# Attention into a gated MLP on one core: outputs of the first and last batch go straight into the MLP's activation tiles, in a newly planned order

## The chip, the cores and the metric

The kernel runs on one NeuronCore of a Trainium2 chip. The metric is the device time of one launch in microseconds (us). Before the change three runs gave 876.30, 876.43 and 876.82 us; the median is 876.43 us.

## The reference

Queries are averaged in pairs of neighbouring positions (1152 positions become 576), attention runs over 4 batches of 8 heads, and the attention outputs, laid out as 2304 tokens of 512 features, go through an MLP with a gate. All is fp32.

```python
q_pool = q.reshape(B, H, S // 2, 2, D).mean(axis=3)          # B, H, S, D = 4, 8, 1152, 64
scores = (q_pool @ k.transpose(0, 1, 3, 2)) / np.sqrt(D)
attn = np.exp(scores - scores.max(-1, keepdims=True))
attn = attn / (attn.sum(-1, keepdims=True) + 1e-9)
x = (attn @ v).transpose(0, 2, 1, 3).reshape(B * S // 2, H * D)   # 2304 x 512
h = x @ w_in                                                  # 512 x 2048
out = (h * np.clip(h + 3, 0, 6) / 6) @ w_out                  # 2048 x 512
```

## The kernel before, in words

**Attention.** Two heads form a pair; there are 16 pairs g (four to a batch), and each is done in two halves h of 288 queries. (15, 1) is thus the second half of the last pair. For a half, TensorE makes the scores (`pv<-qh,kT` for the first five pairs, `pqk` later), ScalarE copies them to SBUF (`s`), VectorE keeps a running maximum (`m`), the maximum is folded and spread over TensorE (`pst`), VectorE subtracts it (`s<-s,pst`, L685), ScalarE takes the exponential (L693), and TensorE multiplies with the values (`pav`, L710). The sums of the exponentials of later pairs are added on GpSimd in four steps for each of the two heads (`d`, L703: two of 864 columns, two of 288); VectorE then folds them (`dh`, L723), TensorE sums over partitions (`psr<-dh,same`, L730, function `sums`), and VectorE inverts, widens and multiplies (`divide`, L781). The result `x` is split into a high part `xh` on ScalarE (L786) and a remainder `xl` on GpSimd (L789), since all matmuls of the MLP work with a high and a low part.

**The way to the MLP.** Each half's `xh` and `xl` (128 x 288) are stored in DRAM (`spill`, L795). The MLP works on chunks of 256 tokens, held feature by feature in `mxh` and `mxl` (`do_load_x`, L382: two loads of 512 KB). The last 768 tokens are done after the attention: a chunk of 256 and a tile `last` of 512 tokens, which `load_last` (L911) fills from DRAM, one pair at a time.

**The MLP.** For each chunk and each of 16 blocks f of the hidden width: `layer` (12 matmuls of 256 columns into `ph`, L392), relu on ScalarE (L397), gate on VectorE (L401), a high part on ScalarE (`gh`, L405) and a remainder on GpSimd (`gl`, L410), and `project` (6 matmuls of 512 columns into `po`, L425). The weights come from `w_d`, where an early conversion put them, two tiles per block (L375), three buffers for each. The second phase's first matmuls need the PSUM that the first five pairs free (the step `second`).

**What sets the order.** `arrange` lists all steps with their needs, buffers, costs and a due place; `Order.run` walks through time with these costs and writes each engine's instructions down in the order it found. On the chip each engine, and the SP queue, which issues nearly all DMAs, follows its own list strictly. START to STICK are the numbers that place the steps.

Of the kernel before, what the change touches and what calls it, by code (L numbers as in the profile page):

```python
# [21 lines left out]
SWEEPS = ((0, 0, 8), (1, 0, 8), (0, 8, 16), (1, 8, 16), (2, 0, 16), (3, 0, 16), (4, 0, 16), (5, 0, 16))  # L22
START = (265.37, 174.4, 333.68, 473.16, 315.93, 125.77, 294.83, 251.1)
SLOPE = (-22.5, 5.61, -19.51, -1.68, 18.53, 29.67, 8.1, 10.68)
LAG = 95.37
MLP = (-455.8, 178.11, 154.5, -337.97)
CONV = 489.51
CSTEP = (779.1, 171.15)
NEAR = 5
EARLY = 5  # L30
FCV = 12
BIAS = (-499.81, -337.54, 74.41, -260.87, -123.47, 36.52)
CUT = 8
PER = (11.97, 20.48)
AT = (268.28, -145.28, 1.89, 285.13, -233.93, 261.99, -360.51, 263.48, 186.09, 367.06, 25.71, -87.67, -226.55, 320.99)
ATL = (21.71, -3.97, -191.36, 678.02, 338.19, 328.75, 109.71, -429.46, 291.22, 244.53, 587.93, 369.41, 499.12, 174.71)
TAIL = 768
STICK = 0.2249
CT = 256
# [8 lines left out]
class Order:  # L48
# [5 lines left out]
    def add(self, key, place, cost, fn, needs=(), takes=(), frees=()):  # L54
        assert key not in self.key, key
        self.key[key] = len(self.steps)
        self.steps.append((round(1e4 * place), cost, fn, tuple(needs), tuple(takes), tuple(frees)))

    def run(self):
# [10 lines left out]
        back, out, t, wires = [], [], 0.0, 0.0  # L70
# [10 lines left out]
        while len(out) < len(steps):  # L81
# [4 lines left out]
            for e in engines:  # L86
# [53 lines left out]
            if not began:  # L140
# [3 lines left out]
                t = min(later)  # L144
        return [(steps[n][2], e) for _, n, e in out]


def arrange(od, do, B=4, NPAIR=4, KT=9, KC=3, NH=2, NFC=16, NT=2304, P=128, HQ=288, SQ=576):
    add = od.add
    chunks = range(0, NT - TAIL, CT)  # L150
    NG, C3 = B * NPAIR, range(KT // KC)

    def place(g):
        return PER[0] * min(g, EARLY) + PER[1] * max(g - EARLY, 0)


    for g in range(NG):
# [34 lines left out]
        for h in range(NH):  # L192
# [75 lines left out]
            add(("dv", g, h), z + at[9], {"DVE": (370, 450)}, do("divide", g=g, h=h), [("rb" if late else "qu", g, h), ("ev", g, h)], (), ("av",))  # L268
            add(("xh", g, h), z + at[10], {"ACT": (340, 420)}, do("split_x", g=g, h=h), [("dv", g, h)], ("xo",))
            add(("xl", g, h), z + at[10], {"POOL": (800, 820)}, do("split_x", g=g, h=h), [("xh", g, h)], (), ("x",))  # L270
            add(("sp", g, h), z + at[10] + 1, {"SP": (940, 5800, 1000)}, do("spill", g=g, h=h), [("xl", g, h)], (), ("xo",))
        add(("lv", g), lead + at[13], {"SP": (470, 5200, 1750)}, do("load_v", g=g), [("lk", g)], ("vr",))
# [18 lines left out]

    def spills(c0, c1):
        return [("sp", b * NPAIR + p, h) for b in range(B) for h in range(NH)
                for p in range(NPAIR) if b * SQ + h * HQ < c1 and b * SQ + (h + 1) * HQ > c0]

    hd = w0 = w1 = pj = None
    after = lambda *keys: [x for x in keys if x]
    for i, (c, f0, f1) in enumerate(SWEEPS):
        for f in range(f0, f1):
            m, first, last = (c, f), f == f0, f == f1 - 1  # L300
            z = START[i] + SLOPE[i] * (f - f0)
            if f == 0:
                add(("lx", c), z - 5, {"SP": (940, 7500, 3100)}, do("do_load_x", c=c), spills(c * CT, (c + 1) * CT), ("mx",))
# [4 lines left out]
            add(("hd", m), z, {"PE": (1440, 1660, 0, "m")}, do("do_layer", m=m), [w0, ("lx", c), ("second",)] + after(hd),  # L308
                ("h",), ("w0",) + (("mx",) if f == NFC - 1 else ()))
# [3 lines left out]
            add(("gh", m), z + MLP[2], {"ACT": (300, 408)}, do("do_upper", m=m), [("ga", m)], ("g",))  # L313
            add(("gl", m), z + MLP[3], {"POOL": (700, 740)}, do("do_lower", m=m), [("gh", m)], (), ("r6",))
# [11 lines left out]
    c = len(chunks)  # L326
    add(("lx", c), place(NG) + 7, {"SP": (940, 7500, 3100)}, do("do_load_x", c=c), spills(c * CT, (c + 1) * CT), ("mx",))
    for p in range(NPAIR):
        add(("ll", p), place(NG - NPAIR + p + 1) + 12, {"SP": (940, 6000, 1550)}, do("load_last", p=p),
            [("sp", NG - NPAIR + p, gr) for gr in range(NH)] + [("sw", NFC - 1, h) for h in range(2)] + ([("ll", p - 1)] if p else []))  # L330
    add(("end", 0), 1e4, {"PE": (1440, 1660, 0, "m")}, do("nothing"), [("lx", c), pj])
    add(("end", 1), 1e4, {"PE": (2730, 2950, 0, "m")}, do("nothing"), [("ll", NPAIR - 1), ("end", 0)])


@with_exitstack
def pooled_attention_then_gated_mlp(ctx, tc, q, k, v, w_in, w_out, out):
# [128 lines left out]
    with ExitStack() as a:  # L465
# [317 lines left out]
        def split_x(eng, g, h):  # L783
            if eng == "ACT":
                xo_t[g, h] = [xo.tile([P, HQ], F32R, tag=t, name=t) for t in ("xh", "xl")]
                nc.scalar.copy(out=xo_t[g, h][0], in_=x_t[g, h])  # L786
            else:
                xh, xl = xo_t[g, h]
                by[eng].tensor_tensor(out=xl, in0=x_t.pop((g, h)), in1=xh.bitcast(F32), op=ALU.subtract)  # L789
# [110 lines left out]
        def do_write(eng, c, t, last):  # L900
# [83 lines left out]
```

## Time and profile before

| | us |
|---|---|
| median of three runs | 876.43 |
| the profiled execution, whole time | 872.62 |
| its span, first to last instruction | 870.8 |
| TensorE (PE) busy | 836.6 |
| VectorE (DVE) busy | 673.8 |
| ScalarE (ACT) busy | 572.3 |
| GpSimd (POOL) busy | 497.8 |

The profiled execution lies 3.8 us under the median. The records call a matmul busy until its result is out, and matmuls overlap, so a busy PE can hide gaps of a fraction of a microsecond. The chain of work that ended last is 74% PE, 12% DVE, 4% DMA, 4% ACT, 4% issue and 2% POOL.

### The profile page before, as it was taken

To read this page: it belongs to the slowest core of one execution; us is meant where nothing else is said; L and a number is where in the kernel's file an instruction comes from. 1 tells how busy PE (TensorE), PEld (TensorE's weight loads), DVE (VectorE), ACT (ScalarE), POOL (GpSimd) and SP (SyncE) were. 2 spreads that over 40 slices of the span, in tenths; PEclk is the share of its full clock that TensorE was granted. 3 is DMA by queue.
4 is the path that set the end of the run, shared out by engine and by line. 5 is a ranking of instruction groups with operands and counts; after the bars stand their busy time and mean duration, and the time that the engine had idled before them with its cause. 6 is when DMAs were issued, how large, how long until landed. Compare 5 with 4: busy or idle time off the path is not lost.

```text
span 870.8 us, 16256 instructions
## 1 busy us (share of the span) xinstructions
PE 836.6 (96%) x5668; PEld 650.8 (75%) x5668; DVE 673.8 (77%) x1330; ACT 572.3 (66%) x1206; POOL 497.8 (57%) x437
## 2 busy tenths in 40 slices
PE   4899999999999999999999999999999999999997
PEld 3445555578878877888887887788888867888886
DVE  3899999998988999988888998899988772222222
ACT  3779889886777777766667876687776652222222
POOL 1658776656777685947686878659684592000000
PEclk9799999999999999999999999999999999999999
DMA  9979586799886868997767778996867678443423
GB/s 239 317 216 285 187 269 227 228 278 361 261 290 219 277 219 255 300 300 267 236 210 240 264 240 259 323 290 207 273 217 244 210 267 269 141 132 117 139 98 95
DMA packets 114545, 206.06 MB, mean 237 GB/s; under 512 B 44576, under 2 KB 68128, under 8 KB 114464
## 3 DMA queue, kind: packets, MB, share of 16 engines
q1 hardware_dynamic: 113776, 203.65, 72.8%
q10 hardware_dynamic: 688, 1.38, 0.6%
q8 instruction: 45, 0.74, 0.3%
q14 instruction: 36, 0.29, 0.1%
HBM read 173.02 MB, written 31.98 MB: 235 GB/s over the span
## 4 chain that ended last, share of the span: by engine, by line
PE 74%; DVE 12%; DMA 4%; ACT 4%; issue 4%; POOL 2%; SPq 1%; DVEq 0%; POOLq 0%; ACTq 0%
PE ph L392 20%; PE po L425 15%; PE pav L710 13%; PE pqk L614 10%; PE pt L425 5%; DVE m L632 4%; PE pv L610 3%; DVE s L685 3%; DMA w<-w_d 2%; ACT s L519 1%; PE pt L588 1%; PE pt L554 1%; PE psr L740 1%; ACT s L693 1%; DMA w_d<-scratch 1%
## 5 line engine op out<-in xcount | busy, mean ns | idle before, releaser
L693 ACT ACTIVATE s<-s 128x864 f32<-128x864 f32 x192 | 177.4, 932 | 21.1 <-DVE s L685 19.0
L392 PE MATMUL ph<-mxmxh,w 128*128 128x256 f32 x896 | 183.1, 287 | 3.3 <-DVE r L401 2.6
L685 DVE TENSOR_TENSOR s<-s,pst 128x864 f32<-128x864 f32 x168 | 174.0, 1042 | 0.4
L519 ACT COPY s<-pqk 128x288 f32<-128x288 f32 x396 | 145.3, 402 | 29.2 <-PE pqk L614 26.2
L710 PE MATMUL pav<-s,vr 128*64 128x288 f32 x1152 | 153.2, 411 | 0.0
L392 PEld LDWEIGHTS ph<-mxmxh,w 128*128 128x128 f32 x896 | 147.6, 192 | 7.3 <-DVE r L401 4.3
L632 DVE TENSOR_TENSOR m<-pqk,m 128x288 f32<-128x288 f32 x308 | 138.0, 448 | 14.8 <-ACT s L519 8.4
L425 PE MATMUL po<-w,gh 128*128 128x512 f32 x448 | 140.1, 394 | 0.0
L397 ACT ACTIVATE r<-ph,three 128x256 f32<-128x256 f32 (+1 forms) x128 | 63.9, 499 | 114.8 <-PE ph L392 110.2
L392 PE MATMUL ph<-mxmxl,w 128*128 128x256 f32 x448 | 127.3, 284 | 0.5 <-DMA mxmxl<-xl_d 0.5
L401 DVE SCALAR_TENSOR_TENSOR r<-r,ph 128x256 f32<-128x256 f32 (+1 forms) x128 | 57.2, 447 | 85.5 <-ACT r L397 84.4
L614 PE MATMUL pqk<-qh,kT 128*128 128x288 f32 x396 | 119.8, 316 | 1.5 <-DVE m L632 0.7
L410 POOL TENSOR_TENSOR gl<-r,gh 128x256 fp32r<-128x256 f32 x96 | 71.4, 745 | 86.9 <-ACT gh L405 70.6
L710 PEld LDWEIGHTS pav<-s,vr 128*64 128x64 f32 x1152 | 77.3, 136 | 57.6 <-issue 9.2
L703 POOL TENSOR_TENSOR d<-s 128x864 f32<-128x864 f32 x44 | 90.6, 2059 | 42.7 <-ACT s L693 42.1
L614 PE MATMUL pqk<-ql,kT 128*128 128x288 f32 x396 | 111.8, 294 | 0.0
L425 PEld LDWEIGHTS po<-w,gh 128*128 128x128 f32 x448 | 84.9, 189 | 14.5
L425 PE MATMUL po<-w,gl 128*128 128x512 f32 x224 | 90.7, 405 | 2.5 <-DMA w<-w_d 2.5
L703 POOL TENSOR_TENSOR d<-d,s 128x864 f32<-128x864 f32 x44 | 90.3, 2052 | 2.9 <-ACT s L693 1.5
L392 PEld LDWEIGHTS ph<-mxmxl,w 128*128 128x128 f32 x448 | 86.0, 192 | 1.7 <-DMA mxmxl<-xl_d 0.8
L614 PEld LDWEIGHTS pqk<-qh,kT 128*128 128x128 f32 x396 | 74.7, 189 | 12.4 <-DVE m L632 3.9
L405 ACT CAST gh<-r 128x256 fp32r<-128x256 f32 (+1 forms) x128 | 55.8, 436 | 37.4 <-DVE r L401 28.0
(104 smaller groups left out, 1412.8 us busy)
## 6 DMA issues: line engine op xcount, KB each, us to landing
w<-w_d SPq DMA_DIRECT2D x224, 512.0 KB, 5.9
w_d<-scratch SPq DMA_DIRECT2D x32, 512.0 KB, 5.6
kr<-in_k_dram SPq DMA_DIRECT2D x32, 288.0 KB, 4.9
vr<-in_v_dram SPq DMA_DIRECT2D x16, 576.0 KB, 4.4
qr<-in_q_dram SPq DMA_DIRECT2D x15, 576.0 KB, 5.6
raw<-in_moe_w_in_dram SPq DMA_DIRECT2D x16, 512.0 KB, 4.7
raw<-in_moe_w_out_dram SPq DMA_DIRECT2D x16, 512.0 KB, 6.0
xh_d<-xh SPq DMA_DIRECT2D x32, 144.0 KB, 4.9
```

The lines of the kernel that those rows point to most:

```text
L392: nc.tensor.matmul(ps, w[:, wi, cs], x[:, c, :], start=(m == 0), stop=(m == 3 * NCC - 1))
L397: nc.scalar.activation(out=r6, in_=ps, func=AF.Relu, bias=three)
L401: nc.vector.scalar_tensor_tensor(out=out, in0=r6, scalar=6.0, in1=ps, op0=ALU.min, op1=ALU.mult)
L410: on.tensor_tensor(out=gl, in0=r6, in1=gh.bitcast(F32), op=ALU.subtract)
L425: nc.tensor.matmul(o, g[:, ts], w[:, wi, :], start=(first and n == 0), stop=(last and n == 2))
L519: nc.scalar.copy(out=out, in_=in_)
L614: nc.tensor.matmul(ps[:, 0:HQ], kT[g][:, j, t, :], w[:, j, :], start=(m == 0), stop=(m == 1))
L632: nc.vector.tensor_tensor(out=m, in0=ps, in1=s0 if t == 1 else m, op=ALU.max)
L685: by[eng].tensor_tensor(out=s, in0=s, in1=m.unsqueeze(1).to_broadcast([P, KC, HQ]), op=ALU.subtract)
L693: nc.scalar.activation(out=s, in_=s, func=AF.Exp, scale=SCALE)
L703: by[eng].tensor_tensor(out=out, in0=x, in1=y, op=ALU.add)
L710: nc.tensor.matmul(av_t[g, h][j * D:(j + 1) * D, :], vr_t[g][:, j, t, :], s_t[g, h][:, j, t, :], start=(t == 0), stop=(t == KT - 1),)
```

## The change

`routes` says for each half which of its 288 columns belong to chunk 0, chunk 1, `last`, or to none of these (then DRAM stays the way). `split_x` writes the pieces for chunks 0 and 1 and for `last` straight into the MLP's tiles. Batch 0 and batch 3 are concerned: of their 16 halves, eight are no longer spilled, and eight spill 64 columns instead of 288; the loads of chunks 0 and 1 and of `last` are gone. Together that is 28 DMAs fewer on SP (477 to 449). Twelve halves are split in two pieces, so ACT and POOL get 12 instructions more each. The needs in `arrange` follow, relus and high parts of the MLP are held in sequence, and all the placing numbers are new.

```diff
+def routes(g, h, NPAIR=4, SQ=576, HQ=288, NT=2304):
+    a = g // NPAIR * SQ + h * HQ
+    cuts = ((0, 0, CT), (1, CT, 2 * CT), (None, 2 * CT, NT - TAIL + CT), ("last", NT - TAIL + CT, NT))
+    return [(x, max(a, c0), min(a + HQ, c1)) for x, c0, c1 in cuts if a < c1 and a + HQ > c0]
...
-START = (265.37, 174.4, 333.68, 473.16, 315.93, 125.77, 294.83, 251.1)
+START = (314.41, 277.67, 359.01, 590.37, 149.89, 253.26, 467.21, 667.81)
...
-            add(("sp", g, h), z + at[10] + 1, {"SP": (940, 5800, 1000)}, do("spill", g=g, h=h), [("xl", g, h)], (), ("xo",))
+            if kept:
+                add(("sp", g, h), z + at[10] + 1, {"SP": (940, 5800, 1000)}, do("spill", g=g, h=h), [("xl", g, h)], (), ("xo",))
...
-            if f == 0:
+            if f == 0 and c > 1:
...
-            add(("re", m), z + MLP[0], {"ACT": (380, 478)}, do("do_relu", m=m), [hd], ("r6",))
+            add(("re", m), z + MLP[0], {"ACT": (380, 478)}, do("do_relu", m=m), [hd] + after(re), ("r6",))
...
         def split_x(eng, g, h):
...
+            for way, c0, c1 in routes(g, h):
+                if way is None:
+                    if eng == "ACT":
+                        xo_t[g, h] = [xo.tile([P, HQ], F32R, tag=t, name=t)[:, 0:c1 - c0] for t in ("xh", "xl")]
+                    xh, xl = xo_t[g, h]
+                else:
...
+                    o = c0 - (NT - TAIL + CT if way == "last" else way * CT)
+                    xh, xl = [x[:, p, o:o + c1 - c0] for x in xs_t[way]]
+                x = x_t[g, h][:, c0 - a:c1 - a]
+                if eng == "ACT":
+                    nc.scalar.copy(out=xh, in_=x)
+                else:
+                    by[eng].tensor_tensor(out=xl, in0=x, in1=xh.bitcast(F32), op=ALU.subtract)
...
-        def load_last(eng, p):
-            if p == 0:
-                xs_t["last"] = [wr.tile([P, NCC, TAIL - CT], F32R, tag=t, name="last", bufs=n) for t, n in (("a", 2), ("b", 1))]
-            for x, d in zip(xs_t["last"], (xh_d, xl_d)):
-                nc.sync.dma_start(out=x[:, p, :].bitcast(F32), in_=d[p, :, NT - TAIL + CT:])
```

The first place is the SP queue at the end of the attention. Before: the spill of (15, 1), the weights of the sixth chunk's last projection (`w_9260`), and the loads of `last`.

```order
L795 DMA xh_d<-xh 128x288
L795 DMA xl_d<-xl 128x288
L375 DMA w_9260<-w_d 128x1024
L911 DMA last<-xh_d 128x512
L911 DMA last<-xl_d 128x512
L375 DMA w_9297<-w_d 128x1024
L375 DMA w_9301<-w_d 128x1024
```

The same stretch of SP now, from the spill of (15, 0), which is 64 columns, on (`w_9216` serves the sixth chunk's last projection).

```order
L822 DMA xh_d<-xh 128x64
L822 DMA xl_d<-xl 128x64
L388 DMA w_9171<-w_d 128x1024
L395 DMA mxmxh<-xh_d 128x4x256
L395 DMA mxmxl<-xl_d 128x4x256
L388 DMA w_9216<-w_d 128x1024
L388 DMA w_9277<-w_d 128x1024
L388 DMA w_9309<-w_d 128x1024
```

No spill and no load of `last` stands between the weights any more.

The second place is GpSimd (POOL) at the same time. Before, from the first of the eight adds of (15, 1) on; the first `xl` is that of (15, 0).

```order
L703 TENSOR_TENSOR d<-s 128x864
L703 TENSOR_TENSOR d<-d,s 128x864
L703 TENSOR_TENSOR d<-d 128x288
L410 TENSOR_TENSOR gl<-r_9095,gh 128x256
L703 TENSOR_TENSOR d<-d 128x288
L703 TENSOR_TENSOR d<-s 128x864
L410 TENSOR_TENSOR gl<-r_9135,gh 128x256
L703 TENSOR_TENSOR d<-d,s 128x864
L789 TENSOR_TENSOR xl<-x,xh 128x288
L703 TENSOR_TENSOR d<-d 128x288 x2
```

Now, from the two pieces of (15, 0) to the end of POOL's list.

```order
L816 TENSOR_TENSOR xl<-x,xh 128x64
L816 TENSOR_TENSOR last<-x,last 128x224
L716 TENSOR_TENSOR d<-s 128x864
L423 TENSOR_TENSOR gl<-r_9134,gh 128x256
L716 TENSOR_TENSOR d<-d,s 128x864
L716 TENSOR_TENSOR d<-s 128x864
L423 TENSOR_TENSOR gl<-r_9182,gh 128x256
L716 TENSOR_TENSOR d<-d 128x288
L716 TENSOR_TENSOR d<-d,s 128x864
L716 TENSOR_TENSOR d<-d 128x288 x3
L816 TENSOR_TENSOR last<-x,last 128x288
```

The remainder of (15, 0) stood behind six of the eight adds of (15, 1) and stands ahead of all of them now. On PE the sum `psr` of (15, 1) now comes right behind this:

```order
L723 MATMUL pav<-s,vr 64x288 x18
L438 MATMUL po_8300<-w_9171,gl 128x512
L438 MATMUL po_8300<-w_9171,gh 128x512 x2
L438 MATMUL po_8301<-w_9171,gl 128x512
L438 MATMUL po_8301<-w_9171,gh 128x512 x2
L743 MATMUL psr<-dh,same 128x18
L438 MATMUL po_8300<-w_9216,gl 128x512
```

Between the `psr` of (15, 0) and this one PE has the `pav` of (15, 1), four projections and two layers; before it had the `pav`, three projections and two layers there.

The third place is PE at the first layer of the MLP. Before and, below it, now:

```order
L680 MATMUL pst<-ident,mq 128x96 x3
L777 MATMUL psr<-ident,rw 128x96 x3
L588 MATMUL pt<-ident,qp 128x96 x6
L554 MATMUL pt<-ident,kr 128x128 x3
L392 MATMUL ph<-mxmxh,w_286 128x256
```

```order
L753 MATMUL psr<-s,ones 32x288 x18
L671 MATMUL pst<-ident,m 96x128 x3
L601 MATMUL pt<-ident,qp 128x96 x6
L405 MATMUL ph<-mxmxh,w_286 128x256
```

The spread of the maximum (`pst<-ident,mq`), which stood two steps ahead of the layer, comes behind it now.

## Rows read from the trace of the kernel before

**Rows 1.** Busy time by stretch: span, PE, PEld, DVE, ACT, POOL, granted clock, DMA share, GB/s.
```profile
0.00:177.50 177.50, 156.43 (x1206) 89.29 (x1207) 155.88 (x255) 141.44 (x238) 109.60 (x105) 0.96 0.80 245
177.50:686.80 509.30, 505.24 (x3526) 414.83 (x3524) 450.37 (x947) 369.70 (x853) 357.74 (x306) 1.00 0.82 264
...
686.80:738.90 52.10, 48.23 (x303) 38.87 (x304) 31.22 (x65) 26.11 (x53) 30.44 (x27) 0.97 0.70 235
738.90:870.80 131.90, 126.71 (x637) 107.78 (x635) 36.38 (x64) 35.07 (x64) 0.00 (x0) 1.00 0.38 122
...
720.20:738.90 18.70, 16.52 (x88) 14.02 (x87) 4.83 (x12) 4.78 (x11) 3.85 (x6) 0.91 0.88 293
```
**Rows 2.** Chain of work that ended last: start us, us, engine, line.
```profile
647.47 1.48 PE po L425 x6
...
727.10 6.49 DMA w<-w_d
733.73 2.86 PE po L425 x6
...
740.46 1.43 PE ph L392 x12
```
**Rows 3.** Timeline of PE, 710 to 734: start us, us, then idle before and its releaser.
```profile
710.63 0.29 PE L730 MATMUL psr<-dh,same 128*128 128x18 f32 x2
...
715.68 4.59 PE L710 MATMUL pav<-s,vr 128*64 128x288 f32 x36
...
723.13 0.29 PE L730 MATMUL psr<-dh,same 128*128 128x18 f32 x2
...
728.31 0.39 PE L392 MATMUL ph<-mxmxl,w 128*128 128x256 f32 x1 [0.51 <-DMA mxmxl<-xl_d]
...
733.73 0.72 PE L425 MATMUL po<-w,gl 128*128 128x512 f32 x1 [1.66 <-DMA w<-w_d]
```
**Rows 4.** Timeline of the SP queue, 726 to 727.
```profile
726.74 0.32 SPq L795 DMA_DIRECT2D xl_d<-xl  x1
```
**Rows 5.** Timeline of POOL, 708 to 724.
```profile
708.28 2.05 POOL L703 TENSOR_TENSOR d<-s 128x864 f32<-128x864 f32 x1 [1.29 <-ACT s L693]
...
719.43 0.80 POOL L789 TENSOR_TENSOR xl<-x,xh 128x288 fp32r<-128x288 f32 x1
720.19 1.69 POOL L703 TENSOR_TENSOR d<-d 128x288 f32<-128x288 f32 x2
723.44 0.74 POOL L410 TENSOR_TENSOR gl<-r,gh 128x256 fp32r<-128x256 f32 x1 [1.56 <-ACT gh L405]
```
**Rows 6.** Timeline of DVE and ACT, 721 to 726.
```profile
721.91 0.48 DVE L723 TRANSPOSE_TENSOR_REDUCE dh<-d 128x9 f32<-128x288 f32 x1 [6.18 <-POOL d L703]
...
725.03 0.47 ACT L397 ACTIVATE r<-ph,three 128x256 f32<-128x256 f32 x1 [1.67 <-PE ph L392]
725.41 0.42 ACT L786 CAST xh<-x 128x288 fp32r<-128x288 f32 x1
```
**Rows 7.** Timeline of PE at the first layer of the MLP.
```profile
176.18 0.46 PE L680 MATMUL pst<-ident,mq 96*128 96x96 f32 x3 [1.03 <-DVE mq L668]
...
177.54 0.56 PE L392 MATMUL ph<-mxmxh,w 128*128 128x256 f32 x1
...
180.25 0.77 PE L658 MATMUL pst<-ident,m 128*96 128x128 f32 x3
```
**Rows 8.** DVE groups by shape: line, operation, count | busy us, mean ns | idle before.
```profile
L685 DVE TENSOR_TENSOR s<-s,pst 128x864 f32<-128x864 f32 x168 | 174.0, 1042 | 0.4
...
L850 DVE TENSOR_TENSOR scratch<-scratch 128x512 fp32r<-128x512 f32 x10 | 11.4, 1140 | 1.5 <-ACT scratch L519 1.2 <-POOL scratch L521 0.3
...
L521 DVE COPY x<-pav 128x288 f32<-128x288 f32 x9 | 4.0, 448 | 0.1
...
L521 DVE COPY qh<-pv 128x576 f32<-128x576 f32 x2 | 1.5, 751 | 4.8 <-PE pv L583 4.8
...
L521 DVE COPY kT<-pv 128x768 f32<-128x768 f32 x1 | 0.9, 944 | 0.0
```

More of the change, by code (lines that the diff above doesn't have):

```diff
@@ L22 @@
 SWEEPS = ((0, 0, 8), (1, 0, 8), (0, 8, 16), (1, 8, 16), (2, 0, 16), (3, 0, 16), (4, 0, 16), (5, 0, 16))
[L23 to L28 removed]
+START = (314.41, 277.67, 359.01, 590.37, 149.89, 253.26, 467.21, 667.81)
+SLOPE = (-5.6, 10.76, -25.02, -56.01, 23.43, 12.72, 33.46, -20.46)
+LAG = 67.58
+MLP = (-259.68, 159.27, -201.52, -629.52)
+CONV = 881.65
+CSTEP = (307.89, -152.66)
 NEAR = 5
[L30 to L32 removed]
+EARLY, FCV = 5, 12
+BIAS = (-507.07, -335.32, -62.8, -498.39, -136.12, 49.46)
 CUT = 8
[L34 to L36 removed]
+PER = (14.96, 19.11)
+AT = (287.28, -63.9, -18.99, 350.55, -352.6, 268.74, -365.42, 298.52, -418.29, 84.92, -151.43, 133.11, -165.98, 531.5)
+ATL = (28.16, -5.7, -192.48, 838.49, 70.05, 352.06, 57.05, -609.05, 385.91, 357.08, 807.22, 507.46, 452.7, 436.29)
 TAIL = 768
[L38 removed]
+STICK = 0.2852
 CT = 256
@@ L268, in arrange @@
             add(("dv", g, h), z + at[9], {"DVE": (370, 450)}, do("divide", g=g, h=h), [("rb" if late else "qu", g, h), ("ev", g, h)], (), ("av",))
-            add(("xh", g, h), z + at[10], {"ACT": (340, 420)}, do("split_x", g=g, h=h), [("dv", g, h)], ("xo",))
-            add(("xl", g, h), z + at[10], {"POOL": (800, 820)}, do("split_x", g=g, h=h), [("xh", g, h)], (), ("x",))
-            add(("sp", g, h), z + at[10] + 1, {"SP": (940, 5800, 1000)}, do("spill", g=g, h=h), [("xl", g, h)], (), ("xo",))
+            ways = routes(g, h)
+            kept = any(x is None for x, _, _ in ways)
+            cost = [sum(int(r * (c1 - c0)) + more for _, c0, c1 in ways) for r, more in ((.94, 65), (2.16, 170))]
+            add(("xh", g, h), z + at[10], {"ACT": (cost[0], cost[0] + 80)}, do("split_x", g=g, h=h),
+                [("dv", g, h)] + [("sw", NFC - 1, n) for n in range(2)] * (g == NG - NPAIR), ("mx", "mx") * (g + h == 0) + ("xo",) * kept)
+            add(("xl", g, h), z + at[10], {"POOL": (cost[1], cost[1] + 20)}, do("split_x", g=g, h=h), [("xh", g, h)], (), ("x",))
+            if kept:
+                add(("sp", g, h), z + at[10] + 1, {"SP": (940, 5800, 1000)}, do("spill", g=g, h=h), [("xl", g, h)], (), ("xo",))
         add(("lv", g), lead + at[13], {"SP": (470, 5200, 1750)}, do("load_v", g=g), [("lk", g)], ("vr",))
@@ L290, in arrange, with spills @@
         + [("cv", f, h, 4) for f in range(FCV) for h in range(2)])
[L292 to L296, printed above, removed]
+    def spills(c):
+        found = []
+        for b in range(B):
+            for h in range(NH):
+                for x, c0, c1 in routes(b * NPAIR, h):
+                    if c0 < (c + 1) * CT and c1 > c * CT:
+                        found += [("sp" if x is None else "xl", b * NPAIR + p, h) for p in range(NPAIR)]
+        return found
+    hd = w0 = w1 = pj = re = gh = None
     after = lambda *keys: [x for x in keys if x]
@@ L301, in arrange @@
             z = START[i] + SLOPE[i] * (f - f0)
[L302 to L303 removed]
+            if f == 0 and c > 1:
+                add(("lx", c), z - 5, {"SP": (940, 7500, 3100)}, do("do_load_x", c=c), spills(c), ("mx",))
             for n in range(2):
@@ L307, in arrange @@
             w0, w1 = ("lw", m, 0), ("lw", m, 1)
-            add(("hd", m), z, {"PE": (1440, 1660, 0, "m")}, do("do_layer", m=m), [w0, ("lx", c), ("second",)] + after(hd),
+            add(("hd", m), z, {"PE": (1440, 1660, 0, "m")}, do("do_layer", m=m), [w0, ("second",)] + ([("lx", c)] if c > 1 else spills(c)) + after(hd),
                 ("h",), ("w0",) + (("mx",) if f == NFC - 1 else ()))
             hd = ("hd", m)
-            add(("re", m), z + MLP[0], {"ACT": (380, 478)}, do("do_relu", m=m), [hd], ("r6",))
+            add(("re", m), z + MLP[0], {"ACT": (380, 478)}, do("do_relu", m=m), [hd] + after(re), ("r6",))
             add(("ga", m), z + MLP[1], {"DVE": (340, 418)}, do("do_gate", m=m), [("re", m)], (), ("h",))
-            add(("gh", m), z + MLP[2], {"ACT": (300, 408)}, do("do_upper", m=m), [("ga", m)], ("g",))
+            add(("gh", m), z + MLP[2], {"ACT": (300, 408)}, do("do_upper", m=m), [("ga", m)] + after(gh), ("g",))
+            re, gh = ("re", m), ("gh", m)
             add(("gl", m), z + MLP[3], {"POOL": (700, 740)}, do("do_lower", m=m), [("gh", m)], (), ("r6",))
@@ L326, in arrange @@
     c = len(chunks)
[L327 to L332, printed above, removed]
+    add(("lx", c), place(NG) - 7, {"SP": (940, 7500, 3100)}, do("do_load_x", c=c), spills(c), ("mx",))
+    add(("end", 0), 1e4, {"PE": (2880, 3100, 0, "m")}, do("nothing"), [("lx", c), pj])
+    add(("end", 1), 1e4, {"PE": (2730, 2950, 0, "m")}, do("nothing"), [("xl", g, h) for g in range(NG - NPAIR, NG) for h in range(NH)] + [("end", 0)])
 @with_exitstack
@@ L783, in split_x @@
         def split_x(eng, g, h):
[L784 to L789, printed above, removed]
+            b, p = divmod(g, NPAIR)
+            a = b * SQ + h * HQ
+            for way, c0, c1 in routes(g, h):
[4 more added lines that the diff above has]
+                else:
+                    if way not in xs_t:
+                        if way == "last":
+                            xs_t[way] = [wr.tile([P, NCC, TAIL - CT], F32R, tag=t, name="last", bufs=n) for t, n in (("a", 2), ("b", 1))]
+                        else:
+                            xs_t[way] = [xp.tile([P, NCC, CT], F32R, tag=t, name="mx" + t) for t in ("mxh", "mxl")]
+                    o = c0 - (NT - TAIL + CT if way == "last" else way * CT)
[3 more added lines that the diff above has]
+                    nc.scalar.copy(out=xh, in_=x)
+                else:
+                    by[eng].tensor_tensor(out=xl, in0=x, in1=xh.bitcast(F32), op=ALU.subtract)
         def spill(eng, g, h):
-            b, p = divmod(g, NPAIR)
-            c0 = b * SQ + h * HQ
+            p = g % NPAIR
+            c0, c1 = [(c0, c1) for way, c0, c1 in routes(g, h) if way is None][0]
             for x, d in zip(xo_t.pop((g, h)), (xh_d, xl_d)):
-                nc.sync.dma_start(out=d[p, :, c0:c0 + HQ], in_=x.bitcast(F32))
+                nc.sync.dma_start(out=d[p, :, c0:c1], in_=x.bitcast(F32))
         raw_t = {}
```

4 lines of the change are left out of this document (2 added, 2 removed).

## The prediction

> **What bounds the kernel now.** I read the table by stretch first, then the chain of waits, then the timelines of the engines where the chain leaves PE. The reader is to see four stretches [rows 1]. Up to 177.5 us PE and DVE are equally busy (156.4 and 155.9 us); the MLP has not begun, and each waits for the other in turn. From there to 686.8 us PE is busy 505.2 of 509.3 us, DVE 450.4, or 88%: PE is the bound, and DVE is close behind. From 686.8 to 738.9 us, the end of the attention, PE is idle for 3.9 us and its clock dips. After 738.9 us PE alone works at full clock, and neither its instructions nor their order differ from before. So the change can act in the first stretch, where the chunks were fetched, in the long middle through a new order, and at the end of the attention, where the spill and the loads of `last` stand on SP.
>
> **The change part by part.** The sum is made against the profiled execution: a span of 870.8 us, 872.6 us with what lies around it. The median of the runs is 3.8 us higher, so I add the differences to 876.43 us.
>
> *A, the waits that go.* The chain of waits shows a weight load of 6.49 us that starts at 727.10 us [rows 2]. SP issued it right after the store of the last `xl` at 726.74 us [rows 4]; in the list it stands behind that store, which needs POOL's remainder, so the load could not go earlier. PE waited 1.66 us for it, and 0.51 us before that for a chunk that was being read back [rows 3]. Behind these waits the granted clock is 0.91 over 18.7 us [rows 1]: 9% of 18.7 us, or 1.7 us of PE's time, since part of the stretch runs at 1.2 GHz instead of 2.4. The six matmuls of the projection that follows show it: 2.86 us, where 1.48 is usual [rows 2]. The new list has no spill and no load between these weights, and the buffer for the weights of the last projection is freed two projections and a `pav` before their use. All of it goes: 0.5 + 1.7 + 1.7 = 3.9 us. Bounds: 0 if the load is late all the same, 3.9 if not.
>
> *B, a wait that comes.* The new list of POOL puts the remainder of (15, 0) ahead of the eight adds of (15, 1). Before, the first of these adds began at 708.28 us [rows 5], 2.4 us ahead of the `psr` of (15, 0) at 710.63 us [rows 3]. Now it comes after a chain that begins with that `psr`. I count from there. On ACT, `xh` stands behind the relu of a layer that PE issues after the `psr`, a projection (1.48) and the layer (1.43, both [rows 2]); with the relu's 0.47 that is 3.4 us. The path through DVE, 2.3 us from `psr` at 723.13 to `xh` at 725.41 [rows 3, 6] and one subtraction of 1.04 [rows 8] in between, takes as long. The two pieces of `xh` cost together about the 0.42 us of the whole, those of `xl` the 0.80: the first add starts 4.6 us after `psr`. The eight adds are four of 2.05 and four of 0.85 (two took 1.69), with two `gl` of 0.74 between them [rows 5]: 8.2 + 3.4 + 1.5 = 13.1 us. `dh` takes 0.48 [rows 6]. So the `psr` of (15, 1) can start 18.2 us after that of (15, 0). PE has beside it four projections (5.9), two layers (2.9) and the `pav` (4.5, from 715.68 on, without the drain [rows 3]): 13.3 us. The wait is 4.9 us. Before, from `psr` to `psr` were 12.5 us with 11.8 of such work, so 0.7 us of waits are there already; 4.2 are new. What is queued behind the waiting `psr` on PE: the sixth chunk's last projection, then the first layer of the final part, so everything. An idle time of this size is longer than those of A, so I charge the same 1.7 us of slow clock behind it. B costs 5.9 us. Bounds: 0, if the adds of (15, 1) find the same head start as before; 5.9 if the count holds, which I take, since each of its terms is a row.
>
> The clock is where I weigh the skill. The row shows a granted clock of 0.91 after idle times of 0.51 and 1.66 us [rows 1, 3]. The Trainium skill, TensorE: Matmul & The Clock Gate, section "What's actually happening", says that the throttled clock is the default and that sustained activity releases it, so a new idle time can bring the half rate back. By that rule B is 5.9 us; if the clock stayed up through a single idle time, B would be 4.2 us and the sum 1.7 us lower. The trace agrees with the rule as far as it goes.
>
> *C, the first layer.* PE now issues it ahead of the spread of a maximum for which it waited 1.03 us, and the twelve matmuls took 2.71 us, from 177.54 to 180.25 us [rows 7], instead of 1.43 [rows 2], at half clock. The chunk is complete without a load. At most 1.0 + 1.3 = 2.3 us go, and nothing if DVE, which is as busy as PE here [rows 1], sets the pace anyway. I take 1.5, nearer to the rows of PE.
>
> *D, work taken off DVE.* By the lists, DVE makes 5 instead of 10 of the weights' remainders (5 of 1.14 us less), two copies of `x` less (0.9), one subtraction more (1.0), two copies of `qh` (1.5) and one of `kT` more (0.9): 5.7 + 0.9 - 1.0 - 1.5 - 0.9 = 3.2 us less [rows 8]. DVE is busy 88% of both long stretches [rows 1]; at that share it is worth 2.8 us. Bounds: 0 to 3.2.
>
> *What I cost at nothing.* Twelve more pieces on ACT and on POOL: ACT is busy 369.7 and POOL 357.7 of 509.3 us in the long middle [rows 1], so each has some 140 us of cover; where they stand on the path, in (15, 0), they are in B. If the cover were gone, twelve pieces at the price of a whole remainder, 0.80 [rows 5], would be at most 9.6 us on POOL. The 28 DMAs that SP no longer issues free its queue all along, but PE's idle time in the long middle is 4.1 us in all, whatever its causes, so beyond A I count no gain. The remainders of the weights that POOL takes over (five more) fall where it has room (109.6 of 177.5 us). The new order of PE's instructions in the middle can gain those 4.1 us or lose as much; both engines' lists hold the same work up to D, and I take 0.
>
> The sum: -3.9 + 5.9 - 1.5 - 2.8 = -2.3 us. The span would be 868.5, the time at the median's level 874.1 us.
>
> **The rivals.**
>
> *The wait at POOL does not come.* If the adds of (15, 1) get ahead of the `psr` of (15, 0) by other waits of PE (any time PE loses between the two `psr` shortens B), A, C and D remain: -8.2 us, 868.2 us. For it: POOL sat idle 1.29 us ahead of the first add before [rows 5], so it had some room. Against it: POOL's list is strict, and 18.2 us of chain against 13.3 of work leave no doubt that something waits.
>
> *POOL times the end of the attention (slower).* The place is the `psr` of the two last halves. If the same chain, remainder first and then the adds, already delays the `psr` of (15, 0), PE idles twice, the clock dips twice (another 1.7 us), and what C and D gained before is only waited off there, since the end is then counted from POOL's list: -3.9 + 5.9 + 1.7 = +3.7 us, 880.1 us. It decides from the point where a half's chain, 18.2 us, exceeds PE's work between two sums; for (15, 0) the gap between `pav` and `pav` was 22 us before, which speaks against it, while q's pooling on POOL and the waits for the exponentials speak for it.
>
> *The transfers were hidden and the early gains are too.* A and a B without the clock's part nearly cancel (-3.9 + 4.2), and DVE's saved time falls where PE is the bound: +0.3 us, 876.7 us.
>
> **How the numbers follow.** A difference under 0.2%, 1.75 us here, is what a measurement of this kernel can't tell from none; faster means under 874.7 us, slower over 878.2. My forecast has 0.48; it has its own range of 872.0 to 876.5, from C and D at their best to both at half, and about 0.30 of it lies under 874.7. The absent wait has 0.15, all faster. The slower rival has 0.25. The hidden transfers have 0.12, of which 0.09 within the bound and 0.03 above it. That makes faster 0.45, same 0.18 + 0.09 = 0.27, slower 0.28. The range of 8 in 10 reaches from 869.0, which leaves out the larger part of the absent wait, to 879.5, which leaves out about half of the slower rival.
>
> **What the profile after would show.** A right: no PE wait for `w<-w_d` of over 0.5 us near the end of the attention. B right: the `psr` of (15, 1) waits for DVE's `dh`, and that for POOL's adds, by 3 to 5 us, with a half clock behind it. C right: the first layer comes at once behind the last score of the fifth pair, at about 175 us, and PE's idle time there shrinks. D right: DVE is busy some 3 us less in all. The forecast is wrong if PE's idle time between 180 and 690 us differs by more than 4 us from the 4.1 of now, for then the new order decides and not these steps; or if the wait at the end falls on the `psr` of (15, 0) too.

## The result, and the profile after

The changed kernel took 880.28 us (879.20 to 882.84, six runs), the kernel before 876.23 us (872.79 to 876.82, six runs): a ratio of 1.0058, 95% interval 1.0037 to 1.0080. It is slower, by about 5 us, where 2.3 us less was forecast. The profiled execution took 879.2 us, with a span of 877.3 us. Here is its busy time by stretch, with the columns of [rows 1] (span; PE, PEld, DVE, ACT and POOL, each with its number of instructions; granted clock; DMA share; GB/s). The stretches end at the same work as there: first layer of the MLP, last half but one, end of the attention.

```profile
0.00:179.00 179.00, 155.13 (x1185) 85.46 (x1186) 156.01 (x251) 141.25 (x245) 108.56 (x109) 0.96 0.76 235
179.00:693.30 514.30, 506.95 (x3558) 416.92 (x3557) 451.04 (x944) 368.65 (x857) 361.05 (x314) 1.00 0.78 253
693.30:745.00 51.70, 46.87 (x293) 38.13 (x292) 32.51 (x69) 25.50 (x56) 30.30 (x28) 0.93 0.60 195
745.00:877.30 132.30, 127.24 (x640) 108.21 (x638) 36.49 (x65) 35.39 (x64) 0.00 (x0) 0.99 0.35 116
```

PE's idle time (span less busy) was 21.1, 4.1 and 3.9 us in the first three stretches of [rows 1]; it is 23.9, 7.4 and 4.8 us now. Of the 7 us more, 6.1 lie ahead of the end of the attention, where I had looked. Two short windows hold 6.0 of them. First of the kernel before, same columns:

```profile
88.00:108.00 20.00, 20.00 (x181) 10.61 (x180) 19.61 (x31) 17.61 (x31) 14.98 (x12) 1.00 0.56 191
186.00:198.00 12.00, 12.00 (x108) 8.24 (x107) 11.47 (x23) 9.79 (x22) 8.15 (x9) 1.00 0.98 272
```

And of the changed kernel:

```profile
88.00:108.00 20.00, 16.60 (x108) 8.89 (x108) 18.04 (x28) 17.41 (x31) 13.79 (x14) 0.91 0.56 183
186.00:198.00 12.00, 9.39 (x66) 6.88 (x63) 11.78 (x13) 9.26 (x20) 10.24 (x10) 0.90 0.86 259
```

*The first window.* PE lost 3.4 us of 20, and its clock fell to 0.91 in this execution. This is the timeline of DVE and PE there (start, length, then in brackets the idle time and what ended it):

```profile
95.62 1.68 PE L723 MATMUL pav<-s,vr 128*64 128x288 f32 x12
...
97.02 2.00 DVE L698 TENSOR_TENSOR s<-s,pst 128x864 f32<-128x864 f32 x2
98.94 0.68 DVE L870 SCALAR_TENSOR_TENSOR scratch<-raw,pv 128x512 uint32<-128x512 uint32 x1
...
99.67 1.02 PE L623 MATMUL pv<-qh,kT 64*128 64x288 f32 x4 [1.70 <-DVE scratch L870]
100.26 0.70 DVE L866 SCALAR_TENSOR_TENSOR pv<-raw,pv 128x512 uint32<-128x512 uint32 x1
...
101.43 2.66 PE L723 MATMUL pav<-s,vr 128*64 128x288 f32 x12
...
104.94 2.02 DVE L698 TENSOR_TENSOR s<-s,pst 128x864 f32<-128x864 f32 x2 [1.28 <-ACT mb L532]
```

The scores and the conversion of weights write to the same three buffers (`pv`). One conversion held a buffer until 99.6 us, because two subtractions of 1.0 us stand in DVE's list ahead of its last step. PE waited 1.70 us for it. Behind that wait twelve matmuls of `pav` took 2.66 us, where 1.68 is usual, and then DVE itself, the busiest engine of this stretch, ran dry for 1.28 us. The wait belongs to the list and the half speed does not: in the repeat of this kernel (e5) PE waits 1.71 us at this place, the twelve matmuls behind it take 1.68 us, DVE goes on without a gap, and the window (that execution is 1.2 us later by then) is at full clock, with 3.7 us lost:

```profile
88.00:108.00 20.00, 16.26 (x121) 8.82 (x114) 19.31 (x30) 17.52 (x31) 14.99 (x15) 1.00 0.54 176
```

*The second window.* This is the timeline of DVE, POOL and PE:

```profile
188.38 1.85 POOL L545 TENSOR_TENSOR qp<-qr 96x768 f32<-96x768 f32 x1
...
189.11 4.87 DVE L877 TENSOR_TENSOR scratch<-scratch 128x512 fp32r<-128x512 f32 x1
...
190.18 1.28 POOL L877 TENSOR_TENSOR scratch<-scratch 128x512 fp32r<-128x512 f32 x1
...
191.41 2.03 POOL L698 TENSOR_TENSOR s<-s,mb 128x864 f32<-128x864 f32 x1
193.38 2.28 POOL L545 TENSOR_TENSOR qp<-qr 96x768 f32<-96x768 f32 x1
...
195.95 0.61 PE L627 MATMUL pqk<-qh,kT 128*128 128x288 f32 x1 [2.61 <-DVE kT L586]
```

One subtraction on DVE, whose shortest fellow takes 0.68 us, lasted 4.87 us: it ended 0.5 us after the third of four POOL instructions that followed each other without a gap. The key tile that PE needed stood behind it in DVE's list.

*The end of the attention.* This is PE's timeline, where [rows 3] had the waits for a chunk and for weights:

```profile
716.57 0.40 PE L743 MATMUL psr<-dh,same 128*128 128x18 f32 x2
...
735.32 0.58 PE L743 MATMUL psr<-dh,same 128*128 128x18 f32 x2 [3.95 <-DVE dh L736]
735.74 0.77 PE L438 MATMUL po<-w,gl 128*128 128x512 f32 x1
...
738.45 0.41 PE L405 MATMUL ph<-mxmxh,w 128*128 128x256 f32 x1
```

And POOL's, for [rows 5]:

```profile
721.04 0.32 POOL L816 TENSOR_TENSOR xl<-x,xh 128x64 fp32r<-128x64 f32 x1 [1.62 <-ACT xh L814]
721.32 0.66 POOL L816 TENSOR_TENSOR last<-x,last 128x224 fp32r<-128x224 f32 x1
722.14 2.07 POOL L716 TENSOR_TENSOR d<-s 128x864 f32<-128x864 f32 x1 [0.16 <-ACT s L706]
...
732.26 2.41 POOL L716 TENSOR_TENSOR d<-d 128x288 f32<-128x288 f32 x3
```

The sums of the last half wait 3.95 us for POOL's adds, as term B has it; the projection behind them takes 2.71 us (735.74 to 738.45) for a usual 1.48.

### The profile page after: what moved, and what is told of

Read it like the earlier page. It is cut to its first block, busy times and chain, and to the rows that moved or that the text cites. A ratio compares the mean times of both kernels' runs of the same rounds, so it can differ in the third digit from the quotient of the medians.

```text
span 877.3 us, 16210 instructions
## 1 busy us (share of the span) xinstructions
PE 836.2 (95%) x5668; PEld 648.7 (74%) x5668; DVE 676.1 (77%) x1327; ACT 570.8 (65%) x1220; POOL 499.9 (57%) x450
## 4 chain that ended last, share of the span: by engine, by line
PE 71%; DVE 13%; ACT 5%; issue 5%; DMA 3%; POOL 3%; SPq 0%; DVEq 0%; POOLq 0%; ACTq 0%
PE ph L405 20%; PE po L438 14%; PE pav L723 12%; PE pqk L627 10%; PE pt L438 5%; DVE m L645 5%; DVE s L698 3%; PE pv L623 2%; POOL d L716 2%; ACT s L532 2%; DMA w<-w_d 2%; ACT s L706 2%; PE psr L753 1%; PE pt L601 1%; PE pt L567 1%
## 5 line engine op out<-in xcount | busy, mean ns | idle before, releaser
L627 PEld LDWEIGHTS pqk<-ql,kT 128*128 128x128 f32 x396 | 75.1, 190 | 2.7
```

What stands on the lines that cost most here:

```text
L627: nc.tensor.matmul(ps[:, 0:HQ], kT[g][:, j, t, :], w[:, j, :], start=(m == 0), stop=(m == 1))
```

## The experiments

My theory after this reading: the routes on chip are not what costs; the new order loses time in three places, in 88 to 108 us, at the 4.87 us instruction, and at the last adds. The rivals: the routes themselves cost it (more pieces, layers that wait for ACT and POOL), or a loss in the first stretch is only moved, since DVE sets that stage's end whatever its order.

To keep all else fixed, the planner's answer is replaced by a written list of (step, engine) in every kernel below. Only the list differs from one to the next, but for one edit of two pool sizes. The list ends where the attention and the sixth chunk end: the matmuls of the final part are not in it. Each ratio is to the kernel before, timed in the same set of runs.

```diff
-        for fn, eng in [(lambda eng: None, None)] + od.run():
+        for fn, eng in [(lambda eng: None, None)] + [(od.steps[od.key[k]][2], e) for k, e in listed(ORDER)]:
```

**e1, the old order with the new routes.**
```diff
-ORDER = the list of the changed kernel
+ORDER = the list of the kernel before, without the steps that are gone (8 of "sp", "lx" 0 and 1, the 4 of "ll")
```


> The changed kernel's code, but every step is issued in the order in which the kernel before issued it (the spills and reloads that the change removes are simply gone). Order theory: the new routes are worth something and the new order loses more. The end then has neither the weight load blocked on SP (0.5), nor the late chunk (1.7), nor the half-speed stretch behind them (1.7): 876.2 - 3.9 = 872.3, between 871 and 874. Routes theory: the extra pieces of the split and the layers that now wait on ScalarE and GpSimd cost the 4 us themselves, whatever the order: 878 or more.

Measured: 0.9985 of before, 0.9970 to 1.0001. So the routes don't cost, and the rival that they do is out; the order costs the rest. But they bring some 1 us, not the 3.9 I expected. The chain of waits at the end of this run (start, length, what) shows why, against [rows 2]:

```profile
723.16 1.39 PE po L438 x6
724.55 0.03 PE psr L743 x2
724.58 7.05 DMA w<-w_d
731.63 0.14 issue
731.76 2.90 PE po L438 x6
```

The spill and the loads of `last` that I had blamed are gone from SP's queue, and the load does leave sooner: 0.2 us behind the `psr` of the last half (724.39 us), where it left 4.0 us behind it before (727.10 against 723.13). But it takes 7.05 us, and PE comes for it sooner too. Of the final part, four matmuls stand ahead of this projection now:

```profile
724.39 0.29 PE L743 MATMUL psr<-dh,same 128*128 128x18 f32 x2
...
729.36 0.41 PE L405 MATMUL ph<-mxmxh,w 128*128 128x256 f32 x2
731.76 0.77 PE L438 MATMUL po<-w,gl 128*128 128x512 f32 x1 [2.00 <-DMA w<-w_d]
```

In the kernel before there were 24, up to this line:

```profile
731.67 0.40 PE L392 MATMUL ph<-mxmxh,w 128*128 128x256 f32 x2
```

So PE reaches the projection 5.4 us behind `psr`, not 8.9, waits 2.00 us, and then runs at half speed. e11 returns to this.

**e2 and e3, one end of the old order each.**
```diff
-ORDER = the list of the changed kernel
+e2: the old list up to ("second",), at about 175 us, then what is left in the new list's order
+e3: the new list up to ("xl", 13, 1), then what is left in the old list's order
```


> The changed kernel, with the order of the kernel before up to the point where the first pass of five pairs is done (about 175 us), and from there the rest in the new order. Order theory: the 5.8 us that TensorE loses at 88 to 108 us, and about 1 us beside it up to 175, do not come: 880.3 - 6.5 = 873.8, between 872.5 and 875.5. Rival, VectorE sets the stage's end whatever its order inside, so what TensorE loses at 88 us it would lose elsewhere before 250 us: 879 to 881.

Measured: 1.0003 (0.9990 to 1.0015). That is 4.8 us below the 1.0058 of the changed kernel, and 6.7 below the 1.0080 of its repeat (e5): the loss of the first stretch is that of its order, and it is not given back later. This list also escapes the second window (PE is busy 11.91 of its 12 us), which the 6.5 expected left out.

> The changed kernel in its new order up to the split of pair 13, from there the rest in the order of the kernel before. Order theory: the scores of the last pair come earlier against the MLP's layers, the adds of the last half start about 12 us before its sums are asked for, so the wait of 3.9 us and the half-speed stretch behind it are gone: TensorE's loss after 700 us falls from 9.4 to about 2 us, less 1.3 that the old order loses at 650 to 700: 880.3 - 6 = 874.3, between 873 and 876. Rival, GpSimd's adds set the end in either order: 879 to 881.

Measured: 1.0186 (1.0161 to 1.0211), against both. Busy time by stretch of this run:

```profile
178.00:690.00 512.00, 497.52 (x3467) 407.44 (x3462) 447.93 (x934) 364.90 (x844) 352.88 (x308) 0.99 0.76 245
690.00:745.00 55.00, 52.18 (x355) 41.31 (x353) 36.71 (x79) 29.98 (x66) 38.29 (x35) 1.00 0.66 223
```

The end is mended (2.8 us idle at full clock, where it was 4.8 us at 0.93), but 14.5 us are lost in the middle, where it was 7.4 with the new list and 4.1 with the old. At the changeover the new list is behind with pair 14: some 60 steps that the old list has issued by then were still to come, and had to be done first. So this run shows that the end's loss belongs to the end's order, and says nothing on its price.

**e4, the long subtraction moved.**
```diff
-("cv", 12, 0, 6) on DVE
+("cv", 12, 0, 6) on POOL, just ahead of ("pq", 6, 0)
```


> The changed kernel with one step moved: the subtraction that ends one weight conversion, on VectorE at 189.11 us for 4.87 us (four others of its kind take 0.68 to 0.9), is done by GpSimd just ahead of its work at 188.4. Lock theory: VectorE stood still because GpSimd ran three reads of on-chip memory back to back and both need the same port; without it VectorE keeps its order and TensorE's wait of 2.6 us behind the key tile at 195.95 is gone: 880.3 - 2.6 = 877.7. Rival, GpSimd is what is short there, and 1.28 us more on it holds the keys as long: 880 to 881.5.

Measured: 1.0063 (1.0042 to 1.0085). PE's wait at the place goes with the instruction, as the lock theory has it; this is the second window in this run:

```profile
186.00:198.00 12.00, 11.69 (x94) 8.28 (x98) 10.02 (x19) 11.10 (x24) 11.21 (x10) 1.00 0.78 227
```

PE is busy 11.69 us instead of 9.39, at clock 1.00. The time does not decide it: against the changed kernel's 1.0058, and 1.0080 in its repeat (e5), the difference is between +0.5 and -1.5 us, with intervals of some 2 us on each. The traces do. Here are the MLP's first relu and its thirteenth, ahead of the place and behind it, in the changed kernel:

```profile
181.25 0.47 ACT L410 ACTIVATE r<-ph,three 128x256 f32<-128x256 f32 x1 [0.58 <-PE ph L405]
...
254.42 0.47 ACT L410 ACTIVATE r<-ph,three 128x256 f32<-128x256 f32 x1
```

And in e4:

```profile
182.71 0.47 ACT L410 ACTIVATE r<-ph,three 128x256 f32<-128x256 f32 x1 [0.58 <-PE ph L405]
...
254.11 0.47 ACT L410 ACTIVATE r<-ph,three 128x256 f32<-128x256 f32 x1
```

This execution of e4 came to the place 1.5 us later (it was as late at 64 us, with the same list) and left it 0.3 us earlier: the instruction cost 1.8 us. PE's wait was 2.61 us; new waits of PE between 200 and 221 us took the rest back.

**e5 to e8, a second set.** e5 is the changed kernel as it is.

> The changed kernel as it is, step for step, so that what follows is compared on one chip: 1.0058 of the kernel before, between 1.004 and 1.008.

Measured: 1.0080 (1.0059 to 1.0100). With the first 1.0058, I take 1.006 to 1.008 for what follows.

```diff
-("cv", 6, 0, 2) and ("cv", 6, 0, 3) ahead of ("su", (2, 0, 0), 2); ("cv", 6, 1, 2) and what needs it ahead of ("mx", (2, 1, 0), 4)
+e6: the first two just behind ("su", (2, 0, 0), 2); the others just behind ("mx", (2, 1, 0), 8)
```


> The changed kernel with two weight conversions moved on VectorE alone, at 94 to 101 us: the three steps of the one are done together, behind the maxima and subtractions that they stood between, and those of the other behind the next five maxima (some 8 us later). TensorE's order is untouched. Place theory: the conversions held one of the three buffers that scores are written into, and stood ahead of maxima that free the others, so that TensorE waited 1.0 and 1.7 us and then ran at half speed: 4 us less than the kernel as it is, between 2.5 and 5.5. Rival, VectorE's total sets the stage, and what is moved behind the maxima delays the next ones by as much: no gain, within 1 us.

Measured: 1.0182 (1.0160 to 1.0203). My edit was bad: conversion (7, 1) now begins before (6, 1) has left the space that they share, so those weights come out wrong. It tells nothing of the theory.

```diff
-ORDER = the list of the changed kernel
+e7: its steps of the MLP's layers behind 600 us sorted in later, by up to 8 us at 690 us
+e8: the same on the list of e2
```


> The changed kernel, with the MLP's layers from 600 us on issued later against the attention, by a lag that grows to 8 us at 690 us: two layers more stand between the last scores and the sums of the last half. Theory that the wait at GpSimd is the loss: the wait of 3.95 us and the half-speed stretch behind it go, 4.5 us less than the kernel as it is. Theory of two waits in one place: the layers' weights are then the last to come, as with the old order (a wait of 2 us and half speed behind it), 1 to 2 us less. Rival, the attention cannot be hurried, because VectorE sets its pace from 600 us on: 0 to 3 us more.

> The old order up to 175 us, and from there the new one with the layers from 600 us on as much later as in the run before. If the two losses lie apart in time they add: the gain of the old early order (4.8 us by its ratio) and that of the later layers (1 to 4.5), so 6 to 9 us less than the kernel as it is, 0.993 to 0.998 of the kernel before. If the early gain were only lent, and given back at the end: no better than the old early order alone, 1.000.

Measured: e7 1.0326 (1.0299 to 1.0353), e8 1.0239 (1.0218 to 1.0260). Both went the rival's way, and further, but not for its reason: from 650 to 700 us of e7 DVE is busy 40.3 of 50 us, less than the 43.2 before the edit, and behind 700 us PE waits 5.3 us for one gate of DVE. The sorting pushed the layers' steps behind attention steps on every engine; that each list then waited for another is my reading, not shown. e8 is still 7.6 us below e7, so the early gain stays even there.

**e9, two adds on another engine.** This touches the end and moves nothing else.
```diff
-("ad", (15, 1, 1), 0) and ("ad", (15, 1, 1), 1) on POOL
+("ad", (15, 1, 1), 0) and ("ad", (15, 1, 1), 1) on DVE, at the same places of the list
```


> The changed kernel, order and all, but the two large adds of the very last unit of probabilities (two of GpSimd's eight behind 722 us, 2.0 us each) are done by VectorE, which stands idle from 726 to 733 us. If GpSimd's chain of adds is what the last sums wait for, they come 2 to 4 us sooner: the wait of 3.95 us before them shrinks to 0 to 2, and 3 to 5 us go from the time (wait and half speed behind it), 0.55 to 0.2 % of it if the two engines can't read on-chip memory side by side. Rival, something behind that wait is due as late (the layers' weights, as with the old order): a new wait of 2 us or more stands there, and no more than 1 us goes.

Measured: 1.0035 (1.0015 to 1.0056), 2 to 4 us below the changed kernel. The timeline of its end:

```profile
730.72 1.55 DVE L716 TENSOR_TENSOR d<-s 128x864 f32<-128x864 f32 x1
731.53 1.33 POOL L423 TENSOR_TENSOR gl<-r,gh 128x256 fp32r<-128x256 f32 x1 [0.17 <-ACT gh L418]
732.38 1.40 DVE L716 TENSOR_TENSOR d<-d,s 128x864 f32<-128x864 f32 x1
732.82 4.11 POOL L716 TENSOR_TENSOR d<-d 128x288 f32<-128x288 f32 x4
...
737.60 0.37 PE L743 MATMUL psr<-dh,same 128*128 128x18 f32 x2 [1.78 <-DVE dh L736]
```

The wait fell from 3.95 to 1.78 us. POOL's chain is the cause, and nothing else was due as late. The next was close: the load of the weights for the projection behind, issued at 729.25 us, took 8.0 us and landed some 0.4 us ahead of the sums. The wait did not vanish: beside DVE's adds `gl` took 1.33 us where 0.74 is usual, and the four small adds 4.11 us where two take 1.69 [rows 5], 1.3 us more in all.

**e10 to e12, the cures together.**
```diff
-ORDER = the list of the changed kernel
+e10: the list of e2, with the two adds of e9 on DVE
+e12: the same, with the pools of e11
```
For e11, the old list with other pool sizes:
```diff
-        w = pool.tile([P, 2, DM], F32R, tag=f"w{n}", name=f"w{n}")
+        w = pool.tile([P, 2, DM], F32R, tag=f"w{n}", name=f"w{n}", bufs=3 + n)
-                        xo_t[g, h] = [xo.tile([P, HQ], F32R, tag=t, name=t)[:, 0:c1 - c0] for t in ("xh", "xl")]
+                        xo_t[g, h] = [xo.tile([P, HQ], F32R, tag=t, name=t, bufs=1)[:, 0:c1 - c0] for t in ("xh", "xl")]
```


> The old order up to 175 us, the new one behind it, and the last two large adds on VectorE. The early gain (1.0058 to 1.0080 down to 1.0003) and that of the adds (3 to 5 us, if theirs is the last wait) lie 600 us apart and add: 0.995 to 0.998 of the kernel before. If either is only lent: 0.999 to 1.002.

Measured: 0.9957 (0.9935 to 0.9979), 870.49 us. The gains of e2 and e9 add. This version beats both kernels.

> The changed kernel in the old order (0.9985 of the kernel before), with four buffers for the second weight of a layer instead of three, and one for the staging of each half of a split instead of two, which makes room. If the wait of 2.0 us for weights at 729.8 us comes from a load that had to wait for its buffer, it goes, and the half speed behind it: 3 to 4 us, 0.994 to 0.996. If it comes from the transfers themselves (four weights of 512 KB and the last chunk's two halves leave within 6 us), the load only starts sooner among the same bytes: under 1 us.

Measured: 0.9967 (0.9947 to 0.9987), with e1's 0.9985 inside its interval. The wait for weights at the end is still 1.54 us, of 2.00: the load left at 721.88 us, 1.4 us ahead of `psr`, and took 7.37 us. So the buffer was not the main cause; that the bytes in flight are, which the other expectation says, fits the 7.05 and 7.37 us of the transfers, but no run changed the bytes.

> Old order to 175 us, new behind it, the two adds on VectorE, four buffers for the second weight. With all three waits away: 0.992 to 0.996 of the kernel before. If the weights' buffer is worth nothing here, as the new order has its weights early: the same as the run with the adds alone.

Measured: 0.9955 (0.9935 to 0.9976), as e10: where the new list stands at the end, the buffer is worth nothing.

**e13 to e15, where in the first stretch.**
```diff
-ORDER = the list of the changed kernel
+e13: the old list up to ("mm", (1, 1, 0), 0), at about 58 us, then the new one
+e14: the old list up to ("s1", (3, 0, 1)), at about 136 us, then the new one
+e15: e14 with the two adds of e9 and the pools of e11
```


> The changed kernel, in the order of the kernel before up to about 58 us, and in the new order from there. Place theory (the loss is that of the maxima and conversions of 88 to 108 us): nothing is cured, TensorE loses 5 to 8 us again in the half that ends at 105 to 108 us, and the time is that of the kernel as it is, 1.005 to 1.009 of the kernel before. Rival, the loss is laid earlier, in what the first 58 us have left undone: 1.000 to 1.003.

> The same with the changeover at about 136 us. Place theory: the loss is gone, as with the changeover at 175 us, 0.998 to 1.002. Rival, the new order carries its loss on to wherever it starts, since it has VectorE convert sooner than the keys need it: 1.004 to 1.008.

Measured: e13 1.0062 (1.0036 to 1.0087): nothing is cured. e14 1.0027 (1.0006 to 1.0048): 3.1 us of it is (the profiled spans are 879.3 and 875.8 us). So the loss of the first window lies between 58 and 136 us; that the held buffer makes it is read from the trace, since e6, which was to test it, tells nothing. But e14 stays 2.1 us above e2, between my two expectations. The two windows in e14:

```profile
88.00:108.00 20.00, 20.00 (x180) 10.76 (x181) 19.61 (x30) 17.78 (x32) 15.56 (x14) 1.00 0.46 159
186.00:198.00 12.00, 9.39 (x65) 6.41 (x67) 11.73 (x15) 8.43 (x19) 7.34 (x6) 0.86 1.01 293
```

The first is clean and the second is back. The group of the subtractions on DVE (shortest, median and longest in ns) in e14:

```profile
L877 DVE TENSOR_TENSOR scratch<-scratch x7: 676/925/4874, 51.5 to 226.6; 128x512 fp32r<-128x512 f32 x7
```

And in e2, whose list makes them at other times:

```profile
L877 DVE TENSOR_TENSOR scratch<-scratch x8: 678/1101/2214, 51.6 to 223.5; 128x512 fp32r<-128x512 f32 x8
```

The list of e14 carries the long instruction, that of e2 does not. The two intervals touch, but the traces place the difference. The same two relus in e14:

```profile
178.26 0.47 ACT L410 ACTIVATE r<-ph,three 128x256 f32<-128x256 f32 x1 [0.58 <-PE ph L405]
...
251.75 0.47 ACT L410 ACTIVATE r<-ph,three 128x256 f32<-128x256 f32 x1
```

And in e2:

```profile
178.37 0.49 ACT L410 ACTIVATE r<-ph,three 128x256 f32<-128x256 f32 x1
...
248.14 0.48 ACT L410 ACTIVATE r<-ph,three 128x256 f32<-128x256 f32 x1
```

The two are level ahead of the place, and e14 is 3.6 us behind after it. The lists differ in more than the one instruction there, so this is the price of the stretch; e4, which moves it alone, gives 1.8 us of that to the instruction.

> The changeover at 136 us, the last two large adds on VectorE, and four buffers for the second weight. The gains lie apart and add: 0.992 to 0.997. If the changeover at 136 us brings its own loss: above 0.998.

Measured: 0.9995 (0.9974 to 1.0016), 3.3 us above e10: it carries the same long instruction (4.87 us in its trace).

## Why the prediction was wrong

*The step that failed* is the one under "what I cost at nothing". The prediction compared the lists of both kernels, found the same work in them up to D, and took 0 for the order, in the long middle; for the first stretch it made no term for the order at all, only the gain C. The runs put a loss of 4.8 us there (e2, against 1.0058; 6.7 against the repeat's 1.0080), made of two places: about 3.1 us between 58 and 136 us (e13, e14), and 2 to 4 us around one held-up instruction (1.8 in e4's trace; 2.1 from e14 to e2, 3.3 from e15 to e10). The sign of the whole hangs on that step. The 4.8 us are counted from the old order of the first stretch, so they take in, for the most part, what C and D gained or failed to gain; beside A and B the sum is then -3.9 + 5.9 + 4.8 = +6.8 us. Measured were +5 to +7 us (1.0058 and 1.0080).

*A: the wait went, its 3.9 us did not.* No wait for `w<-w_d` stands at the end now. SP's queue did hold the load up, as e1 shows, where it leaves 3.8 us sooner against the `psr`; but it is long as well (7.05 us there, 6.49 in [rows 2]), and how late it comes hangs on where PE wants it, which the sum took as fixed. In the changed kernel the load behind the chunk's two halves (the weights of the last projection) left at 725.00 us and took 7.6 us to land, at 732.6. PE had come to the `psr` ahead of that projection at 731.4 us: without B's wait it would have stood some 1.2 us for the weights (an estimate from these times). The two were not separate terms; they are one place, at which PE waits for whichever comes last.

*B: right.* From `psr` to `psr` 18.75 us against 18.2; the first add 5.6 us after the first of them against 4.6; the wait 3.95 us, with 4.9 in all predicted. The half speed behind it cost 2.4 us (2.71 for 1.48 in the projection, 2.56 for 1.43 in the layer that follows, 738.45 to 741.01) against 1.7. e9 shows that POOL's chain is the cause. The clock behaved as the sentence of the Trainium skill that I weighed says (TensorE: Matmul & The Clock Gate, section "What's actually happening"), 0.93 in that stretch. Not every idle time brought the half rate: in the first window of e5 the clock stayed at 1.00 behind the wait of 1.71 us.

*C: right at its place, but not seen in the time.* Behind the fifth pair's scores PE waits 0.16 us instead of 1.03, and its clock is 1.00 from 176 to 180 us. But it had lost 3.4 us in the first window, and the layer began at 179.54 us instead of 177.54 [rows 7]; my 175 us was wrong for the same reason.

*D: wrong mostly by one instruction.* DVE makes 5 remainders as counted, but they took 8.1 us and not 5.7, for the one of 4.87 us. DVE's busy time rose from 673.9 to 676.1 us (sums of the stretches), where 3 us less was to be seen; with that instruction at its fellows' 0.7 to 0.9 us it would have fallen by some 2 us. What a microsecond off DVE is worth in the time, which D put at its busy share of 88%, no run shows.

*The rivals.* The time came out at the slower rival's 880.1 us, but by another mechanism: there was no wait at the `psr` of (15, 0), and only one dip of the clock at the end. The test that I set for the order, 4 us of PE's idle time between 180 and 690 us, was no help: it rose by 3.3 us in the first execution and by 4.3 in the repeat. It looked past the stretch where the order cost most.

What stays open: how much the routes are worth by themselves (e1 says between 0 and 2.6 us), and what makes up the 3.8 us by which e10 beats the kernel before.

## What to carry to other kernels

When a change comes with a new order, price the order stretch by stretch, and first where two engines are equally busy: each step that holds a shared buffer or stands in one list ahead of what the other engine needs can cost a wait there that no count of work shows. Two waits at one place are one term: taking one away uncovers the other. A cure that touches two steps (e9) could be read, and a shift of whole lists (e3, e7, e8) brought its own losses.

## What the hardware showed that was not expected

DVE's subtraction with both inputs in on-chip memory took 4873 ns once, where the shortest takes 682. It began at 189.11 us, beside a POOL instruction that read on-chip memory until 190.23; the two POOL instructions that began at 190.18 and 191.41 us went ahead of it as well. It is no accident: in all nine profiled kernels with the same list at that place (the changed one, e3, e5, e6, e7, e9, e13, e14, e15) it took 4860 to 4878 ns. That POOL's reads held it up is read from these times; no run moved them. Nor does it always come so: in e2 a subtraction of this form, begun at 186.52 us beside the same POOL step, took 1.55 us, and POOL's next step 1.73 us for 1.28. The Trainium skill, SBUF — State Buffer, section "Who interferes with whom", says that a VectorE instruction with two inputs there contends with GpSimd's reads. The same page of the Trainium skill, section "SBUF: two separate sides", says that whoever starts first holds the port for the whole instruction. The traces agree that one holds the other up; in the changed kernel the waiting one was not even the next. POOL pays too: in e9, beside DVE's adds, its `gl` took 1.33 us for 0.74.
